# A convolution and two-layer feed-forward kernel on one core: w_in in three pieces, half 1's x by casting DMAs, the casts moved, seven blocks in halves

## The chip, the cores and the metric

One core of one Trainium2 chip. The metric is the device time of one execution, in microseconds (us). The kernel before: 693.57 us, median of three runs (692.63 to 694.27). PE is the matmul engine and PEld its weight load, DVE is VectorE, ACT ScalarE, POOL GpSimd, SP SyncE.

## The reference

```python
# x: (8, 4096, 192), weight: (8, 7), w_in: (192, 2048), w_out: (2048, 192)
w = softmax(weight, axis=-1)                      # 8 heads, 7 taps
x_pad = concat([zeros(8, 6, 192), x], axis=1)     # causal, padded in front
conv[b, s, h, :] = sum_k w[h, k] * x_pad[b, s + k, h, :]       # 24 channels a head
h = conv.reshape(32768, 192) @ w_in
out = maximum(0.01 * h, h) @ w_out                # (32768, 192), float32
```

## The kernel before

The 32768 rows are 32 blocks; a block is 512 positions of two batches (e = 0 and 1, one on each half of the partitions). For a block, VectorE convolves (three channel chunks c, seven taps each), PE multiplies by w_in (`mm1`, into the PSUM tile ph), ScalarE applies the leaky ReLU (into g), and PE multiplies g by w_out (`mm2`, into po), one group of blocks later. The first `NHALF` blocks go as two half groups of 256 positions each, so that the first matmuls can start early. A unit is the `mm1` work that fills one ph tile (in a half group, two of the 16 column groups of w_in, so that units 0 to 3 use its first half and units 4 to 7 its last); a step is two units and a share of `mm2`, four steps to a half group and eight to a full block.

In the head, before any of that runs, the softmax weights are made and block 0 is brought in by halves (q = 0 to 3 are the four halves of blocks 0 and 1). Two of half 0's three chunks are convolved on PE, with diagonal "tap matrices" (`diag`), and only the third on VectorE.

```python
    NHALF = 5                                  # blocks that go in halves
    groups = [(b, h * HT, HT) for b in range(NHALF) for h in range(2)]
    groups += [(b, 0, ST) for b in range(NHALF, NBLK)]
# [cut]
    def load_first(q):                         # [cut to its branches]
        # q 0, 1: float32 into x_nat on SyncE's queue (1 with rows interleaved), cast later on ACT or DVE
        # q 2:    casting DMA on GpSimd's queue into x_rows;   q 3: casting DMAs in chunks into x_half
# [cut]
    load_first(0)
    load_first(1)
# [cut: sel, built on GpSimd]
    w_in = [const_pool.tile([128, NCH, F // 2], BF16, name=f"w_in{h}") for h in range(2)]
    load_w_in(0, 0)                            # casting DMAs on GpSimd's queue, 64 partitions each
    ident = const_pool.tile([128, 128], BF16)
    make_identity(nc, ident)
    load_w_in(0, 1)
    for e in range(2):
        load_w_in(1, e)
    load_first(2)
    # then w_out, load_first(3), load_x(2), on the same queue
# [cut]
    select(wps_hm, slice(0, 2))                # tap weights: high and middle parts
    warm(3)                                    # matmuls on zeros
    select(wps_l, 2)                           # low part, another bank of the same tile
    warm(7)
    warm(1, 128)
    nc.vector.tensor_copy(out=whm, in_=wps_hm)
    diag_wide(0, 0, K)                         # tap matrices on VectorE
    cast_first(0, 0, nc.vector.tensor_copy)
    diag_low(0, range(2))                      # tap matrices on ScalarE
    cast_first(0, 1, nc.scalar.copy)
    transpose_first(0)
    warm(3)
# [cut: scalars, evacuation of half 0, the other tap matrices, the convolution of half 0]
        for u in range(2 * j, 2 * j + 2):
            mm1(grp, u)                        # unit u: two of the 16 column groups of w_in
            if i == 0 and u == 0:
                transpose_first(1)
                evac_first(1, nc.vector.tensor_copy, nc.vector.tensor_copy)
```

## Time and profile before

| | before |
|---|---|
| median time, span of the profiled run | 693.57 us, 692.1 us |
| PE busy | 684.0 us |
| first mm1 matmul that is not held up by w_in | 11.68 us |
| first mm2 matmul | 22.63 us |
| first full block starts, the next one | 116.18 us, 134.35 us |
| the last 160 mm2 matmuls start | 677.15 us |

A line of a timeline has the start in us, how long the group lasted from its first to its last instruction, the engine, the source line, what is written and read, the count, and in brackets the idle time just before it with what ended it. The timeline of GpSimd shows the queue of casting loads. A load is issued only after the load eight places before it has landed, so the waits tell landings:

```profile
1.86 0.76 POOL L253 DMA_DIRECT2D w_in<-in_moe_w_in_dram  x1
...
3.15 1.90 POOL L253 DMA_DIRECT2D w_in<-in_moe_w_in_dram  x3
...
9.63 0.72 POOL L134 DMA_DIRECT2D x_half<-in_x_dram  x1 [1.68 <-DMA w_in<-in_moe_w_in_dram]
11.92 0.72 POOL L134 DMA_DIRECT2D x_half<-in_x_dram  x1 [1.57 <-DMA w_in<-in_moe_w_in_dram]
13.81 0.72 POOL L134 DMA_DIRECT2D x_half<-in_x_dram  x1 [1.17 <-DMA w_in<-in_moe_w_in_dram]
15.67 1.43 POOL L134 DMA_DIRECT2D x_half<-in_x_dram  x2 [1.14 <-DMA w_in<-in_moe_w_in_dram]
```

The four loads of w_in landed a quarter microsecond before these lines: at about 9.4, 11.6, 13.5 and 15.4.

### The profile page before, as it was taken

The page shows a single profiled execution, that of the slowest core. Times are in us where ns is not written, and L with a number is a line of the kernel's source. Part 1 is how long each engine was busy: PE and PEld are TensorE (multiplying, and loading weights), DVE is VectorE, ACT ScalarE, POOL GpSimd, SP SyncE. Part 2 cuts the span into 40 slices and gives each one's busy share as a digit, 9 for nine tenths or more (in the row PEclk, how much of TensorE's full clock was granted, in tenths as well). Part 3 has the DMA queues.
Part 4 walks back from the last instruction along what each step waited for, and adds up shares of the span by engine and source line. Part 5 has one row for each costly group of instructions (what it writes and reads, how often), then busy time and mean ns, then how long its engine had stood idle before and what let it go on. Part 6 is the DMA issues. An engine that isn't in the chain of part 4 may idle for free.

```text
span 692.1 us, 26111 instructions
## 1 busy us (share of the span) xinstructions
PE 684.0 (99%) x11798; PEld 584.3 (84%) x11798; DVE 543.6 (79%) x1001; ACT 516.6 (75%) x575; POOL 144.6 (21%) x202
## 2 busy tenths in 40 slices
PE   8999999999999999999999999999999999999998
PEld 6999998788888888888888888888888888888887
DVE  6999999877878787878787878877878878787812
ACT  6888888977777777777777777777777777777771
POOL 6722220502222202222102222102222012000000
PEclk9999999999999999999999999999999999999999
DMA  9966644935565355566445565455665355222112
GB/s 181 107 84 94 83 70 71 93 71 75 66 93 81 69 81 72 71 90 85 68 76 76 75 82 85 73 76 70 83 81 79 74 74 67 70 60 59 48 42 65
DMA packets 183456, 54.00 MB, mean 78 GB/s; under 512 B 148528, under 2 KB 182576, under 8 KB 183344
## 3 DMA queue, kind: packets, MB, share of 16 engines
q0 software_dynamic: 98576, 14.56, 29.7%
q1 hardware_dynamic: 84768, 37.77, 23.0%
q8 instruction: 92, 1.51, 0.9%
q14 instruction: 20, 0.16, 0.1%
HBM read 29.88 MB, written 25.17 MB: 80 GB/s over the span
## 4 chain that ended last, share of the span: by engine, by line
PE 82%; DVE 14%; DMA 1%; ACT 1%; issue 1%; POOL 0%; POOLq 0%
PE po L432 42%; PE ph L403 40%; DVE yt L201 13%; DMA w_in<-in_moe_w_in_dram 1%; DVE yt L195 1%; ACT g L413 1%; DVE xt L176 0%; POOL w_in L253 0%; POOL sel L242 0%; DVE o_sb L479 0%; POOL sel L240 0%; PE ptr L156 0%; POOL ident masks.py:199 0%; POOL ident masks.py:197 0%; POOLq masks.py:199 0%
## 5 line engine op out<-in xcount | busy, mean ns | idle before, releaser
L413 ACT ACTIVATE g<-ph 128x1024 bf16<-128x1024 f32 x512 | 496.4, 1021 | 154.8 <-PE ph L403 154.3
L201 DVE SCALAR_TENSOR_TENSOR yt<-xt,wk,yt 128x512 bf16<-128x512 bf16 (+1 forms) x648 | 442.5, 683 | 17.7
L432 PEld LDWEIGHTS <-g 64*128 64x128 bf16 (+1 forms) x8064 | 361.0, 94 | 33.9 <-issue 0.2
L432 PE MATMUL po<-w_out,g 64*128 64x192 bf16 (+1 forms) x8064 | 387.5, 243 | 0.0
L403 PE MATMUL ph<-yt,w_in 64*128 64x512 bf16 (+1 forms) x3552 | 384.3, 347 | 3.1 <-DVE yt L201 1.3
L403 PEld LDWEIGHTS <-w_in 64*128 64x128 bf16 x3552 | 228.3, 111 | 65.7 <-issue 5.4
L79 POOL DMA_DIRECT2D x_bf<-in_x_dram x180 | 133.9, 770 | 427.1 <-DMA xt<-x_bf 318.1
L479 DVE COPY o_sb<-po 128x192 f32<-128x192 f32 x216 | 77.2, 358 | 122.6 <-PE po L432 115.6
L195 DVE TENSOR_SCALAR yt<-xt,wk 128x512 bf16<-128x512 bf16 (+1 forms) x108 | 38.4, 356 | 0.6 <-PE ph L403 0.5
L479 ACT COPY o_sb<-po 128x192 f32<-128x192 f32 x40 | 12.8, 320 | 2.1 <-PE po L432 0.2
L280 PE MATMUL warm<-zero 128*128 128x256 bf16 (+1 forms) x26 | 4.9, 340 | 1.1 <-DVE junk L237 1.1
L220 PE MATMUL acc<-xt,diag 64*64 64x256 bf16 x84 | 5.4, 271 | 0.4 <-ACT diag L342 0.4
L134 POOL DMA_DIRECT2D x_half<-in_x_dram x6 | 4.3, 714 | 5.6 <-DMA w_in<-in_moe_w_in_dram 5.6
L220 PEld LDWEIGHTS <-diag 64*64 64x64 bf16 x84 | 4.3, 106 | 1.3 <-DVE xt L176 0.6
L342 ACT ACTIVATE diag<-ident,whm 128x64 bf16<-128x64 bf16 x11 | 2.8, 339 | 2.1 <-DVE whm L328 2.1
L280 PEld LDWEIGHTS <-zero 128*128 128x128 bf16 x26 | 2.7, 118 | 2.1 <-DVE junk L237 1.1
L176 DVE COPY xt<-ptr 128x384 bf16<-128x384 bf16 x7 | 2.6, 416 | 1.4 <-PE ptr L156 1.4
L253 POOL DMA_DIRECT2D w_in<-in_moe_w_in_dram x4 | 2.7, 667 | 0.0
L368 ACT ACTIVATE yt<-acc,rsum 128x256 bf16<-128x256 f32 x3 | 1.4, 469 | 0.7 <-PE acc L220 0.7
L286 ACT ACT_TABLE_LOAD x1 | 1.3, 1283 | 0.8 <-PEq L572 0.8
L156 PE MATMUL ptr<-ident,x_half 64*128 64x64 bf16 x36 | 1.2, 190 | 0.6 <-DVE wraw L354 0.6
L140 ACT CAST x_half<-x_nat 128x384 bf16<-128x384 f32 x3 | 1.5, 503 | 0.3 <-DMA x_nat<-in_x_dram 0.3
(37 smaller groups left out, 13.0 us busy)
## 6 DMA issues: line engine op xcount, KB each, us to landing
out_dram<-o_sb SPq DMA_DIRECT2D x118, 192.0 KB, 2.1
x_bf<-in_x_dram POOLq DMA_DIRECT2D x180, 64.0 KB, 3.2
out_dram<-o_sb SPq DMA_DIRECT2D x20, 96.0 KB, 1.6
w_in<-in_moe_w_in_dram POOLq DMA_DIRECT2D x4, 384.0 KB, 9.1
xt<-x_bf SPq DMA_TRANSPOSE x90, 2.5
w_out<-in_moe_w_out_dram POOLq DMA_DIRECT2D x1, 768.0 KB, 13.7
x_nat<-in_x_dram SPq DMA_DIRECT2D x2, 192.0 KB, 2.5
x_nat<-in_x_dram SPq DMA_DIRECT2D x1, 384.0 KB, 7.5
```

The source lines that it names most:

```text
L79: nc.gpsimd.dma_start(out=t[:, c, :, e, :], in_=src[2 * rp + e, :, :, c * CH : (c + 1) * CH],)
L134: nc.gpsimd.dma_start(out=x_half[q][:, c, :, e, :], in_=rows[:, e, :, c * CH : (c + 1) * CH],)
L195: lambda s=src, d=dst, c=c: nc.vector.tensor_scalar_mul(d, s, wk[:, c, 0:1])
L201: lambda s=src, d=dst, c=c, k=k: nc.vector.scalar_tensor_tensor(out=d, in0=s, scalar=wk[:, c, k : k + 1], in1=d, op0=mybir.AluOpType.mult, ...
L220: lambda k=k, p=p, a=a, e=e, ps=ps: nc.tensor.matmul(out=acc[ps, :T], lhsT=diag[c][ps, p, k, :], rhs=xt[0][ps, c, a : a + T], start=(k == ...
L253: nc.gpsimd.dma_start(out=w_in[half][e * CH : (e + 1) * CH], in_=moe_w_in[:, fs].rearrange("(c p) f -> p c f", p=CH),)
L280: nc.tensor.matmul(out=wa[:, 0, 0:cols], lhsT=zero[:, 0:128], rhs=zero[:, 0:cols], start=True, stop=True,)
L342: nc.scalar.activation(out=diag[c][:, 1, k, :], in_=ident2, func=mybir.ActivationFunctionType.Copy, scale=whm[:, c, 1, k : k + 1],)
L403: nc.tensor.matmul(out=ph[:, e, i * T : (i + 1) * T], lhsT=w_in[f * 2 // NFC][ps, c, f // RUN % 2 * RUN * 128 + f % RUN : (f // RUN % 2 + ...
L413: act = nc.scalar.activation(out=g[blk][:, nf * u : nf * (u + 1), :, t0 : t0 + T], in_=ph.rearrange("p e (i t) -> p i e t", i=nf), func=my ...
L432: return nc.tensor.matmul(out=po[m], lhsT=g[b][ps, fc, e, s * 128 : (s + 1) * 128], rhs=w_out[ps, fc, :], start=start, stop=stop,)
L479: ins = copy(out=o_sb[:, n % 2, :], in_=po.pop(n))
```

## The change

The intent: get w_in's first columns sooner (a quarter instead of a half), take half 1's x and its casts away from ScalarE, do half 0's casts before anything that depends on the tap weights, and give VectorE four more half groups, in which it gains on PE, before the first full convolution.

```diff
-    NHALF = 5
+    NHALF = 7
 [cut: half 1 now takes half 2's path, a casting DMA into x_rows, then 24 transposes; its interleaved layout goes]
     load_first(0)
-    load_first(1)
 [cut]
-    w_in = [const_pool.tile([128, NCH, F // 2], BF16, name=f"w_in{h}") for h in range(2)]
+    pieces = (0, NFC // 4, NFC // 2, NFC)
+    w_in = [
+        const_pool.tile([128, NCH, (b - a) * 128], BF16, name=f"w_in{a}")
+        for a, b in zip(pieces[:-1], pieces[1:])
+    ]
 [cut: load_w_in and the slices of mm1 follow]
     load_w_in(0, 1)
-    for e in range(2):
-        load_w_in(1, e)
+    load_first(1)
+    for n in (1, 2):
+        for e in range(2):
+            load_w_in(n, e)
     load_first(2)
 [cut]
-    wps_l = wps[:, 1, 0 : NCH * (K + 1)].rearrange("p (c k) -> p c k", c=NCH)
+    wps_l = psum_o.tile([128, NCH, K + 1], FP32, name="wps_l", tag="po")
     select(wps_hm, slice(0, 2))
-    warm(3)
+    warm(1, 128)
     select(wps_l, 2)
-    warm(7)
-    warm(1, 128)
+    warm(6)
 [cut]
     diag_wide(0, 0, K)
-    cast_first(0, 0, nc.vector.tensor_copy)
+    for e in range(2):
+        cast_first(0, e, nc.scalar.copy)
     diag_low(0, range(2))
-    cast_first(0, 1, nc.scalar.copy)
     transpose_first(0)
 [cut: half 0 evacuated ahead of one small product; three tap matrices from VectorE to ScalarE;
       half 1's casts on ScalarE go; two more outputs are stored singly]
-                if i == 0 and u == 0:
+                if i == 0 and u == 1:
                     transpose_first(1)
```

More of the change, by code (lines that the diff above doesn't have):

```diff
@@ L43 @@
     NBLK = (B // 2) * NB
-    NHALF = 5
+    NHALF = 7
     RUN = 4
-    RUNS = 1
     NPEC = 2
@@ L109 @@
     x_half = {
-        q: const_pool.tile([128, NCH, HS, 2, CH], BF16, name=f"x_half{q}") for q in (0, 1, 3)
+        q: const_pool.tile([128, NCH, HS, 2, CH], BF16, name=f"x_half{q}") for q in (0, 3)
     }
-    x_rows = const_pool.tile([128, 2, HS, D], BF16, name="x_rows")
+    x_rows = {
+        q: const_pool.tile([128, 2, HS, D], BF16, name=f"x_rows{q}") for q in (1, 2)
+    }
     def load_first(q):
-        rows = x[0:2, q * HT : (q + 1) * HT, :].rearrange(
-            "e (p s) d -> p e s d" if q == RUNS else "e (s p) d -> p e s d", s=HS
-        )
-        if q < 2:
+        rows = x[0:2, q * HT : (q + 1) * HT, :].rearrange("e (s p) d -> p e s d", s=HS)
+        if q == 0:
             x_nat[q] = stage_pool.tile([128, 2, HS, D], FP32, name="x_nat")
-            if q == RUNS:
-                nc.sync.dma_start(
-                    out=x_nat[q].rearrange("p e s d -> p e (s d)"),
-                    in_=rows.rearrange("p e s d -> p e (s d)"),
-                )
-                return
             for e in range(2):
                 nc.sync.dma_start(out=x_nat[q][:, e], in_=rows[:, e])
-        elif q == 2:
+        elif q in x_rows:
             for e in range(2):
-                nc.gpsimd.dma_start(out=x_rows[:, e], in_=rows[:, e])
+                nc.gpsimd.dma_start(out=x_rows[q][:, e], in_=rows[:, e])
         else:
@@ L154, in transpose_first @@
                     ps = slice(i * CH, (i + 1) * CH)
-                    if q != 2:
+                    if q in x_half:
                         nc.tensor.transpose(
@@ L164, in transpose_first @@
                             out=ts[i][e * CH : (e + 1) * CH, s, c, :],
-                            in_=x_rows[ps, e, s, c * CH : (c + 1) * CH],
+                            in_=x_rows[q][ps, e, s, c * CH : (c + 1) * CH],
                             identity=ident[ps, ps],
@@ L171, in evac_first @@
         dst = xt[0][:, :, HALO + q * HT : HALO + (q + 1) * HT].rearrange(
-            "p c (i k s) -> p i s c k" if q == RUNS else "p c (s i k) -> p i s c k",
-            s=HS, i=2,
+            "p c (s i k) -> p i s c k", s=HS, i=2
         )
@@ L246, with load_w_in, w_in_of @@
         )
-    w_in = [const_pool.tile([128, NCH, F // 2], BF16, name=f"w_in{h}") for h in range(2)]
-    def load_w_in(half, e):
-        fs = slice(half * F // 2, (half + 1) * F // 2)
+    pieces = (0, NFC // 4, NFC // 2, NFC)
[3 more added lines that the diff above has]
+    ]
+    def load_w_in(n, e):
+        fs = slice(pieces[n] * 128, pieces[n + 1] * 128)
         nc.gpsimd.dma_start(
-            out=w_in[half][e * CH : (e + 1) * CH],
+            out=w_in[n][e * CH : (e + 1) * CH],
             in_=moe_w_in[:, fs].rearrange("(c p) f -> p c f", p=CH),
         )
+    def w_in_of(f, ps, c):
+        n = max(n for n in range(3) if pieces[n] <= f)
+        a = (f // RUN * RUN - pieces[n]) * 128 + f % RUN
+        return w_in[n][ps, c, a : a - f % RUN + RUN * 128 : RUN]
     load_w_in(0, 0)
@@ L358 @@
     nc.vector.reciprocal(rsum, rsum)
+    evac_first(0, nc.vector.tensor_copy, nc.scalar.copy)
     wk = const_pool.tile([128, NCH, K], FP32, name="wk")
     nc.vector.tensor_mul(wk, wraw[:, :, 0:K], rsum.to_broadcast([128, NCH, K]))
-    evac_first(0, nc.vector.tensor_copy, nc.scalar.copy)
     diag_low(0, range(2, K))
     diag_wide(1, 0, K)
-    diag_wide(1, 1, 3)
-    diag_low(1, range(3, K))
+    diag_low(1, range(K))
     def act_scale(out, in_, scale):
@@ L378 @@
         evac_y(act_scale)
-        cast_first(1, c, nc.scalar.copy)
         if c == 0:
@@ L390 @@
     LAST = NSUB - 2 * SUB
-    SINGLE = LAST - 12
+    SINGLE = LAST - 14
     def mm1(grp, u):
@@ L404, in mm1 @@
                         out=ph[:, e, i * T : (i + 1) * T],
-                        lhsT=w_in[f * 2 // NFC][
-                            ps, c, f // RUN % 2 * RUN * 128 + f % RUN
-                            : (f // RUN % 2 + 1) * RUN * 128 : RUN
-                        ],
+                        lhsT=w_in_of(f, ps, c),
                         rhs=y[ps, c, t0 : t0 + T],
```

## The prediction

> **What bounds the kernel now.** I read the page's busy shares and chain first, then the chain in order of time, then the timelines of the first 16 us and of the stretch around 116 us.
>
> ```profile
> PE 684.0 (99%) x11798; PEld 584.3 (84%) x11798; DVE 543.6 (79%) x1001; ACT 516.6 (75%) x575; POOL 144.6 (21%) x202
> ...
> PE 82%; DVE 14%; DMA 1%; ACT 1%; issue 1%; POOL 0%; POOLq 0%
> ```
>
> The kernel is a stream of matmuls. Work that the change doesn't touch sets most of the time: a full block needs 8 steps of 2.615 us (134.35 to 155.27 us in the timeline holds 8 steps: 20.92 us), and 32 such blocks are 669 us. The other 24 us of the 693.57 are the head before the first block, places where PE waits, and a tail. Only these can be won. The 14% of VectorE in the chain lie all before 118.5 us: up to there the convolution on VectorE runs without a pause, and PE keeps barely behind it.
>
> The chain in order of time, at the head:
>
> ```profile
> 3.15 8.48 DMA w_in<-in_moe_w_in_dram
> 11.63 0.05 issue
> 11.68 0.76 PE ph L403 x11
> 12.44 0.17 PE ptr L156 x8
> ...
> 12.72 1.06 DVE xt L176 x2
> 13.79 0.02 issue
> 13.81 0.30 DVE yt L195
> ```
>
> First matmuls of block 0 wait for the first half of w_in until 11.63; the transposes of half 1 stand behind them, and VectorE, done with half 0 at 11.3, sits until 12.71 for those transposes. But the load hides other work that ends just as late (timeline of the head):
>
> ```profile
> 4.64 0.21 DVE L328 COPY whm<-wps 128x48 f32<-128x48 f32 x1 [1.03 <-PE wps L316]
> 4.88 0.62 DVE L334 TENSOR_TENSOR diag<-ident,whm 128x448 bf16<-128x448 bf16 x1
> ...
> 5.37 0.49 ACT L140 CAST x_half<-x_nat 128x384 bf16<-128x384 f32 x1
> 5.42 0.54 DVE L140 CAST x_half<-x_nat 128x384 bf16<-128x384 f32 x1
> ...
> 8.23 3.09 DVE L201 SCALAR_TENSOR_TENSOR yt<-xt,wk,yt 128x256 bf16<-128x256 bf16 x6
> ...
> 10.99 0.47 ACT L368 ACTIVATE yt<-acc,rsum 128x256 bf16<-128x256 f32 x1 [0.71 <-PE acc L220]
> ```
>
> Even with w_in there at once, the second tap sum leaves ACT at 11.46 and VectorE's third of half 0 at 11.3: an earlier w_in **alone** is worth 0.2 us. The rest must come from the casts and tap matrices.
>
> The second place is the passage from half blocks to full ones (timeline of PE):
>
> ```profile
> 113.55 1.51 PE L403 MATMUL ph<-yt,w_in 64*128 64x256 bf16 x24
> 114.86 1.52 PE L432 MATMUL po<-w_out,g 64*128 64x192 bf16 x32
> 116.18 0.63 PE L403 MATMUL ph<-yt,w_in 64*128 64x512 bf16 x4
> 118.08 1.06 PE L403 MATMUL ph<-yt,w_in 64*128 64x512 bf16 x8 [1.27 <-DVE yt L201]
> ```
>
> PE stands 1.27 us for the first full convolution. The VectorE timeline has it starting at 102.81, its thirds at 107.97 and 112.95, and the end at 118.0: 15.2 us for a full one, while the last half group before it gives PE only four steps of 2.63 us, 10.52. VectorE had a lead of 105.66-102.81 = 2.85 us and needed 1.27 more.
>
> **What the Trainium skill says.** "TensorE: Matmul & The Clock Gate", Back-to-back issue gap: an isolated gap of N/2.4+2.5 ns when warm: 109 ns for 256 columns, 216 for 512. Here two row tiles run as a pair; 24 half matmuls take 1.31 us (113.55 to 114.86), 109 ns a pair, and 12 full ones 1.30 us (134.35 to 135.65), 216 a pair. The trace agrees, and going in halves costs PE only the 2.5 ns twice. "VectorE: DVE Perf Modes", The TRN2 errata: ops from SBUF pay a fixed extra latency per instruction. Here six 256-wide taps last 3.09 us (0.52 each), six 512-wide 4.69 us (0.78); the fixed part is 2x0.52-0.78 = 0.26 us, so halves burden VectorE. "DMA: Bandwidth & Descriptors", SWDGE vs HWDGE vs iDMA: a cast during a DMA goes only by GpSimd's path. So half 1's x now queues among w_in's pieces. Same page, Specifications: below 512 B a transfer loses line rate. The x rows land as 384 B, yet the trace shows little of it: last w_in piece at 4.41+11.0 = 15.4, both x_rows by 5.77+10.7 = 16.5, so 192 KB in about 1.1 us, against about 2.0 us for 384 KB of w_in (landings at 9.4, 11.6, 13.5, 15.4).
>
> **The change part by part.**
> 1. *Tap weights.* wps_l gets a tile of its own. Now the copy of whm waits 1.03 us for both selections, which share one tile; the first ended at 3.6 (3.26+0.33). The copy can go at 3.65, 1.0 us earlier; tap matrix 3.9 to 4.5, then four small ops (0.83 us together, from 5.89 to 6.72 now) until 5.4.
> 2. *Casts first.* Both go to ACT ahead of the tap matrices. x lands at about 3.8 and 4.3 (issues at 1.27 and 1.7 plus the 2.5 us in the DMA issues), so casts at 3.8 to 4.3 and 4.3 to 4.8 (0.50 each), the transposes at 4.9 to 5.3 (now 6.08 to 6.46), evacuated by 5.95 on ACT. PE's tap sums then start at 5.95 instead of 7.25 and last 3.7 us: 9.7 to 9.9. VectorE does its scalars, one tap matrix (0.62) and starts its third at 6.6 instead of 7.91: done at 10.0.
> 3. *ACT's load.* Three more tap matrices than now (14 against 11, 0.25 us each in a row), but half 1's two casts go (0.5 each), of which one stood between the two scalings. ACT: 12 tap matrices from 5.95 to 8.95, first scaling 9.4, second 9.9 to 10.4. So matmuls run freely from 10.45 instead of 11.68: **1.2 us earlier**.
> 4. *w_in in pieces.* Until 9.7 the queues now move 768 KB of x and 384 of w_in, some 0.18 MB/us from 3.0 on. With half as much of each, quarter 0 lands at about 7.3 (an estimate), half 1's x at 8.4, quarter 1 at 10.4, the last half at 14.4, half 2's x at 15.5, w_out at 19.2 (now 20.2). Needed at 10.5, 11.8, 12.3, 14.5, 18 and 21: in time, only the last half of w_in is tight.
> 5. *Half 1's transposes after two units.* Units of 0.66 us: 10.45 to 11.75, transposes (24, 0.38 us as half 2's now) to 12.1, copies 0.61 (half 2's now) instead of 1.06, whose target was interleaved. VectorE restarts convolving at 12.75 instead of 13.81: **1.05 us earlier**, and the first group that it bounds starts at 19.5 instead of 20.5. ACT's eight activations (0.98 each) have the same lead. From here PE and VectorE both run about **1.1 us** ahead of before.
> 6. *Seven blocks in halves.* Four more half groups. A convolution of a half takes 10.22, 10.22, 9.96, 9.97, 10.12 and 9.97 us in groups 4 to 9 (mean 10.08), PE 10.52: 0.44 us of lead each, 1.76 in all. Shortfall 1.27, so the wait at the passage goes, with 0.5 to spare. ACT's gap there falls from 1.75 us to its usual 0.33: **1.4 us** won. The passage itself (ACT bound for one block) stays. Cost: 16 steps of 2.630 instead of 2.615: 0.24 us.
> 7. *SINGLE.* One more pair of outputs goes out singly; SyncE isn't on the path: 0.
>
> Sum: 693.57 - 1.1 - 1.4 + 0.24 = **691.3 us**.
>
> **The rivals.**
> (a) *w_in's last half comes late.* Quarters mean 2 KB reads and 1 KB writes, and half 1's x is ahead of them; if it lands at 15.5, unit 4 waits 1 us and ACT idles. But VectorE's end at 19.5 hides about 0.5 of it. Head gain 0.5: 691.9.
> (b) *ACT's chain doesn't move.* If x lands late or its 14 tap matrices outlast the plan, units start at 11.0 or later and, as two stand ahead of the transposes instead of one, VectorE restarts hardly earlier: head gain 0.3: 692.1. For it: ACT is named in the waits of the head; against: it has gaps of 0.7 us at 10.3 and 0.65 at 5.9 now.
> (c) *The wait at the passage stays,* as VectorE gains less per half than I count (GpSimd's issues stretch its first op from 0.28 to 0.53). At 0.25 us a group the wait shrinks to 0.3: 691.6.
> (d) *More:* the lead at the head also removes the idle bits that PE has up to 22 us; perhaps 0.7 us: 690.6.
>
> **Range and chances.** Best case of all parts gives about 690, only the passage or only the head about 692.4; the runs of before spread by 1.6 us. So 690.1 to 692.7. No path moves 2% (14 us).
>
> **What would show it.** Right: matmuls with w_in starting at 10.2 to 10.8 and no wait on w_in after; VectorE's first op of half 1 near 12.8; no wait of PE on VectorE at the first full block (near 157 us); half steps of 2.63 us. Wrong: a wait on w_in at unit 2 or 4, VectorE idle over 1.5 us around 11, a wait of PE over 0.5 us at the passage, or a new idle stretch at w_out's first use near 21 us.

## The result

The changed kernel took 693.19 us (median of four runs, 692.58 to 694.74), the kernel before 693.83 us beside it; ratio 0.9997, 95% interval 0.9975 to 1.0018. In a later job with five more rounds it was 693.04 against 694.15, ratio 0.9988 (0.997 to 1.0005). A ratio is the mean time of one kernel's fast runs over that of the other's of the same rounds, so not quite the ratio of the medians. The profiled run has a span of 691.1 us, 1.0 less than before.

| | before | after | difference |
|---|---|---|---|
| first mm1 matmul that waits for nothing of half 0 | 11.68 | 11.18 | -0.50 |
| VectorE starts convolving half 1 | 13.81 | 13.59 | -0.22 |
| first mm2 matmul | 22.63 | 22.85 | +0.22 |
| first full block: from its start to the next one's | 18.17 | 16.71 | -1.46 |
| the last 160 mm2 matmuls start | 677.15 | 676.13 | -1.02 |

The sum closes: +0.22 in the head, -1.46 in the first full block, +0.24 for two blocks in halves (four half groups of 10.52 us for two full blocks of 20.92) make -1.00, against the -1.02 of the last line. The passage gave what was forecast. The head, forecast at -1.1, gave nothing.

The page of the changed kernel, its busy shares and its chain, by engine and by line:

```profile
PE 684.8 (99%) x11998; PEld 596.9 (86%) x11998; DVE 546.4 (79%) x1025; ACT 521.9 (76%) x593; POOL 147.2 (21%) x206
...
PE 96%; DMA 1%; ACT 1%; POOL 1%; issue 0%; DVE 0%; POOLq 0%
```

VectorE's 14% of the chain have gone to PE: VectorE is no longer behind anything. But the span moved by 0.15%. A chain's shares tell what was waited for last, not how long the waiting was: VectorE had been only just behind.

The chain in order of time, at the head:

```profile
7.09 9.69 DMA w_in<-in_moe_w_in_dram
16.78 0.05 issue
16.83 1.50 PE ph L402 x23
18.33 0.88 PE acc L212 x14
...
21.12 1.03 ACT g L409
22.15 0.04 issue
22.20 0.85 PE ph L402 x12
23.04 1.32 PE po L428 x32
```

Before, a load of w_in ended at 11.63 and VectorE set the pace from there. Now the chain waits for the *last* piece of w_in until 16.78, and 6.0 us after that the first mm2 matmul runs (22.85). The timeline of PE says the same, and shows a second loss ahead of it:

```profile
3.99 1.46 PE L282 MATMUL warm<-zero 128*128 128x256 bf16 x6
5.38 0.50 PE L149 MATMUL ptr<-ident,x_half 64*128 64x64 bf16 x12
5.81 0.82 PE L282 MATMUL warm<-zero 128*128 128x256 bf16 x3
6.56 2.07 PE L212 MATMUL acc<-xt,diag 64*64 64x256 bf16 x28
8.56 0.39 PE L282 MATMUL warm<-zero 128*128 128x256 bf16 x2
8.89 1.72 PE L212 MATMUL acc<-xt,diag 64*64 64x256 bf16 x28
...
16.83 1.50 PE L402 MATMUL ph<-yt,w_in 64*128 64x256 bf16 x23 [1.18 <-DMA w_in<-in_moe_w_in_dram]
```

The same three warm-up matmuls last 0.50 us in the kernel before (at 6.40) and 0.82 us here, the same 12 transposes 0.35 and 0.50, the same 28 tap sums 1.72 (at 7.25) and 2.07; the next 28 last 1.72 again. So PE was at a slow clock until about 7 us here and had left it by 4.5 to 5 before. The Trainium skill, "TensorE: Matmul & The Clock Gate", What's actually happening, says that PE starts at half its clock and is released after a busy window of some 3.4 us whose phase is not tied to the kernel. The durations fit such a halving. The cores view, a mean of 1.000 in both, does not show it, but the clock records kept with the traces do (not a view; in times from the span's start): the full clock was granted from 4.60 us in the kernel before, while the first trace of the changed kernel has no record. The window shows too: between two changes the clock stayed full for a whole number of 3.413 us (4 and 197 in casts_late below, 200 to 202 in the others).

The passage, timeline of PE; there is no wait where 1.27 us stood:

```profile
155.84 1.50 PE L402 MATMUL ph<-yt,w_in 64*128 64x256 bf16 x24
158.47 1.49 PE L402 MATMUL ph<-yt,w_in 64*128 64x512 bf16 x12
160.43 1.76 PE L402 MATMUL ph<-yt,w_in 64*128 64x512 bf16 x12
```

### The profile page after: what moved, and what is told of

The parts are those of the page before. It is cut to its first block, busy times and chain, and to the rows that moved or that the text cites. A ratio compares the mean times of both kernels' runs of the same rounds, so it can differ in the third digit from the quotient of the medians.

```text
span 691.1 us, 26558 instructions
## 1 busy us (share of the span) xinstructions
PE 684.8 (99%) x11998; PEld 596.9 (86%) x11998; DVE 546.4 (79%) x1025; ACT 521.9 (76%) x593; POOL 147.2 (21%) x206
## 3 DMA queue, kind: packets, MB, share of 16 engines
q1 hardware_dynamic: 84512, 37.38, 22.3%
## 4 chain that ended last, share of the span: by engine, by line
PE 96%; DMA 1%; ACT 1%; POOL 1%; issue 0%; DVE 0%; POOLq 0%
PE po L428 49%; PE ph L402 47%; DMA w_in<-in_moe_w_in_dram 1%; ACT g L409 1%; POOL w_in L248 0%; POOL x_rows L123 0%; PE acc L212 0%; POOL sel L233 0%; DVE o_sb L475 0%; PE ptr L156 0%; POOL ident masks.py:199 0%; POOL sel L231 0%; POOL ident masks.py:197 0%; PE ptr L149 0%; POOLq masks.py:199 0%
## 5 line engine op out<-in xcount | busy, mean ns | idle before, releaser
L193 DVE SCALAR_TENSOR_TENSOR yt<-xt,wk,yt 128x512 bf16<-128x512 bf16 (+1 forms) x684 | 450.5, 659 | 19.4
L402 PEld LDWEIGHTS <-w_in 64*128 64x128 bf16 x3744 | 240.6, 111 | 56.8 <-issue 3.2
L475 DVE COPY o_sb<-po 128x192 f32<-128x192 f32 x200 | 71.5, 358 | 113.7 <-PE po L428 108.0
L475 ACT COPY o_sb<-po 128x192 f32<-128x192 f32 x56 | 17.9, 319 | 3.1 <-PE po L428 0.2
L123 POOL DMA_DIRECT2D x_rows<-in_x_dram x4 | 2.9, 734 | 0.4 <-DMA w_in<-in_moe_w_in_dram 0.4
```

Source lines behind the costliest of these rows:

```text
L193: lambda s=src, d=dst, c=c, k=k: nc.vector.scalar_tensor_tensor(out=d, in0=s, scalar=wk[:, c, k : k + 1], in1=d, op0=mybir.AluOpType.mult, ...
L402: nc.tensor.matmul(out=ph[:, e, i * T : (i + 1) * T], lhsT=w_in_of(f, ps, c), rhs=y[ps, c, t0 : t0 + T], start=(c == 0), stop=(c == NCH - 1),)
L475: ins = copy(out=o_sb[:, n % 2, :], in_=po.pop(n))
```

## The experiments

Twelve runs were made, of ten new kernels (the changed kernel and halves came twice), in three jobs on three chips, each with the kernel before in its rounds. All were correct. The theories after the result: **load** (w_in's last half comes late, by smaller rows or by what is queued ahead of it), **clock** (PE is at its slow clock for longer), **passage** (seven blocks in halves win 1.2 us, whatever the head does). "Tap sums" is how long the first 28 took, 1.72 at full clock. "Last w_in" is the last load's issue plus its time to landing. "Wait" is PE's in all for w_in. "Full clock" is when the trace's clock records first have it (- where a trace has no record).

| run | median us | ratio to before | tap sums | last w_in | wait | first mm2 | full clock |
|---|---|---|---|---|---|---|---|
| before | 693.57 | | 1.72 | 15.4 | 0.5 | 22.63 | 4.60 |
| before7 | 693.58 | 0.9995 (0.9982 to 1.0007) | 1.72 | 16.6 | 1.5 | 23.67 | 6.33 |
| after | 693.19 | 0.9997 (0.9975 to 1.0018) | 2.07 | 16.8 | 1.2 | 22.85 | - |
| after_again | 693.04 | 0.9988 (0.997 to 1.0005) | 3.19 | 16.7 | 0 | 24.73 | 12.32 |
| nhalf5 | 693.41 | 0.9989 (0.9977 to 1.0002) | 3.06 | 16.7 | 0.2 | 23.01 | 9.36 |
| x1_sync | 693.1 | 0.9988 (0.9976 to 1.0001) | 2.14 | 15.8 | 0 | 22.16 | 7.46 |
| both | 693.95 | 1.0 (0.9983 to 1.0018) | 2.99 | 16.4 | 0 | 23.02 | 9.22 |
| warm | 693.22 | 0.9986 (0.9969 to 1.0003) | 1.72 | 17.4 | 1.8 | 23.49 | 5.18 |
| halves | 692.24 | 0.9977 (0.9963 to 0.9991) | 2.62 | 15.8 | 0 | 23.38 | 9.26 |
| halves_again | 692.92 | 0.9986 (0.9971 to 1.0001) | 3.19 | 16.2 | 0 | 23.40 | 10.02 |
| halves_warm | 692.2 | 0.9977 (0.9966 to 0.9989) | 1.72 | 16.0 | 0 | 22.45 | - |
| hwarm_u0 | 692.39 | 0.9977 (0.9966 to 0.9989) | 1.72 | 15.7 | 0 | 22.12 | 5.80 |
| casts_late | 692.67 | 0.9996 (0.9978 to 1.0015) | 1.72 | 17.7 | 2.5 | 25.42 | 4.48 |
| halves_early | 696.2 | 1.0026 (1.0011 to 1.0042) | 3.19 | 14.3 | 0 | 26.07 | 13.46 |

A profile is of one run; the spans of one kernel in one job differ by up to 3.9 us (the kernel before in after_again's job: 691.0 to 694.9), so one row's head is not a median's.

### The passage: nhalf5 and before7

```diff
 nhalf5, on the changed kernel          before7, on the kernel before
-    NHALF = 7                          -    NHALF = 5
+    NHALF = 5                          +    NHALF = 7
```

> The changed kernel with five blocks in halves instead of seven. If the passage is what seven blocks win: PE waits about 0.9 to 1.3 us for VectorE at the first full block near 116 us again, and the span is 0.7 to 1.2 us longer than the changed kernel's, about 692. Rival (the wait would have gone through the head's change alone): no wait there, span about 690.9.

> The kernel before with seven blocks in halves, nothing else. If the passage alone carries the gain: no wait of PE at the first full block near 158 us, the passage block 16.7 us instead of 18.2, 0.24 us paid for the longer steps, span about 690.9, or 1.2 us less than the kernel before's, as good as the whole change or 0.2 better. Rival (halves gain nothing without the new head): a wait over 0.5 us stays.

Timeline of PE in nhalf5: the wait is back.

```profile
116.56 0.63 PE L402 MATMUL ph<-yt,w_in 64*128 64x512 bf16 x4
118.21 1.06 PE L402 MATMUL ph<-yt,w_in 64*128 64x512 bf16 x8 [1.02 <-DVE yt L193]
```

In before7 it is gone: the first full block starts at 159.30 with no idle time ahead of its matmuls. Its start is 135.63 us after the first mm2 matmul, and 135.62 in the changed kernel, so the stretch from there is the same with either head. Its span is only 0.2 us shorter than that of the kernel before, as in this run the first half of w_in came 1.0 us later (PE waits 1.54 us for it, until 12.72) and took back what the passage gave. So the passage theory holds in the traces, and in all of them: from the first mm2 matmul to the last 160 it is 653.3 to 653.9 us in the twelve profiles with seven blocks in halves, 654.3 and 654.5 in the two with five. The times don't show it: before7's spans average 691.9 against 692.3 for the kernel before in the same rounds, not 1.2 less, and nhalf5's average 691.5, the changed kernel's ten 691.6. Why the unprofiled runs show so little of it is open.

### The load: halves, halves_again, x1_sync, both

```diff
 halves, halves_again
-    pieces = (0, NFC // 4, NFC // 2, NFC)
+    pieces = (0, NFC // 2, NFC)
-    for n in (1, 2):
+    for n in (1,):
 x1_sync: half 1's x as before (SyncE's queue, float32, ScalarE casts), w_in in quarters and a half
     load_first(0)
+    load_first(1)
 both: halves and x1_sync together
```

> The changed kernel with w_in in two halves again, all else kept. Small-rows theory (a quarter writes 1 KB rows and moves at some 110 to 130 KB/us, a half writes 2 KB rows at some 190): the first half lands at about 8.5 us, half 1's x at 9.6, the last half at about 14 instead of 16.8, so the matmuls with w_in have no wait of 1.2 us on it; the first mm2 matmul comes at about 21.8 instead of 22.85 and the span falls by about 1 us to about 690. Queue-order theory (half 1's x ahead of the rest of w_in makes it late): the last half still lands at 16 or later and the wait stays.

> The changed kernel with w_in in two halves, once more, for comparison in the same rounds. If packets of 2 KB for 1 KB are what w_in gains: last half by 15.9 again, no wait of PE on w_in; ratio to the kernel before 0.997 to 0.9985 and a span of 690.3 to 691.9, the longer ones where x comes late or the clock is slow. If the first time was luck: ratio 0.999 or more.

> The changed kernel with half 1's x as fp32 through SyncE's queue and cast on ACT as in the kernel before, w_in still in quarters and a half. Queue-order theory: without the 192 KB of x ahead of it w_in's last half lands 1.1 to 1.6 us sooner, 15.2 to 15.7, and the wait of 1.2 us at unit 4 shrinks to 0.3 or less. Small-rows theory: the quarters stay slow and twice the bytes of x share the engines, so the last half lands at 16.5 to 18 and the wait stays at 1 us or more; the span is the changed kernel's or up to 1 us more.

> The changed kernel with all of its loads undone: w_in in two halves and half 1's x through SyncE and cast on ACT; the casts ahead of the tap matrices, the two units ahead of the transposes and seven blocks in halves stay. If the loads set the head: the first half of w_in lands at 11.3 to 12.7 as in the kernel before, the matmuls with w_in wait for it, no wait on the last half, and the first mm2 matmul comes at 22.3 to 23.7, no sooner than before; span 690.8 to 692. If the reordered compute gains by itself: first mm2 matmul at 21.8 or sooner, span about 690.3.

With w_in in two halves the last half landed at 15.8, 16.2, 16.0 and 15.7 in four profiles, with quarters at 16.8, 16.7, 16.7, 17.4 and 17.7 in five: means of 15.9 and 17.1. PE waits for w_in in four of the five and in none of the four; the late clock hides a wait in both runs of halves, but hwarm_u0, whose free matmuls start at 11.27 as against the changed kernel's 11.18, has none either. The forecasts of 8.5 and 14 were too early even so (the first half landed at 10.3), and the first mm2 matmul, forecast at 21.8, came at 23.38. halves_again's ratio, 0.9986, lies between the two bands that were forecast.

The 1.2 us are lost ahead of the last half: the first half and half 1's x had landed by 11.6 to 12.4, the two quarters and x by 12.4 to 13.7. Why quarters are slower is shown only in part. In the trace's DMA packets (not a view, but counted from its records) the two quarters are 768 packets of 1 KB, of 114 to 125 ns each on average. The first half, in the same place of the queue, is 384 packets of 2 KB, of 208 to 237 ns. (In the last half, later, 2 KB take only 174 to 178.) Over 16 DMA engines that is about 5.7 us (768 x 119 / 16) against 5.3 (384 x 222 / 16), 0.4 of the 1.2, and a rough estimate, as the busy share of an engine goes up to 1.4 there, so that packets overlap. That quarters are also six loads instead of four was not tested apart.

x1_sync goes against the small-rows theory as it stood: with the quarters kept, and only half 1's x out of GpSimd's queue, the last half landed at 15.8 and PE's wait was gone, nearly what the queue-order theory said. Timeline of PE, where the wait of 1.18 us stood:

```profile
14.83 2.81 PE L413 MATMUL ph<-yt,w_in 64*128 64x256 bf16 x36
```

In the changed kernel half 1's x landed 1.0 us after the first quarter (9.6 after 8.6), and 1.0 us is what its going gave. So **either** undoing removed the wait (x1_sync in its one profile); together, in both, the loads landed no sooner (16.4, and 15.4 and 16.6 in the two kernels with the old loads). Why they don't add is open; the old loads alone scatter by 1.2 us. There is also a limit that I had not counted: GpSimd's queue is slow at first. In two profiles of the changed kernel it moves 75 to 190 KB/us from 4 to 9 us, with SyncE's queue empty, and about 200 only from 12 us on; in the kernel before it moves 84 to 137 from 4 to 8 us with SyncE's moving 49 to 123 beside it, and about 200 from 10 on. The engines were not left idle by the x taken off SyncE's queue: from 4 to 9 us their busy share was 0.86 to 1.38 in the changed kernel's first trace and 0.95 to 1.11 in the kernel before. They moved fewer bytes in that time.

both gained nothing (ratio 1.0), with the new order of compute and with seven blocks in halves. That fits the theory that the loads set the head only in part: the wait for the first half, forecast with it, did not come, as that half landed at 11.2 and the late clock (tap sums of 2.99 us) let the free matmuls start at 12.10 only.

### The clock: after_again, warm, halves_warm

```diff
 warm, on the changed kernel; halves_warm, on halves
     select(wps_hm, slice(0, 2))
-    warm(1, 128)
+    warm(3)
     select(wps_l, 2)
-    warm(6)
+    warm(7)
+    warm(1, 128)
```

> The changed kernel once more, for a ratio over five rounds and a second look at its head. If the first result was typical: ratio to the kernel before 0.998 to 1.000, span 690.5 to 692.5, the last half of w_in lands at 16.2 to 17.2 and PE waits for it at unit 4 unless its first unit is late, and PE's tap sums still start at the slow clock (28 of them in 2.0 us or more against 1.72). If that was bad luck: tap sums in 1.75 us or less, w_in's last half before 15.8, span under 690.5.

> The changed kernel with the warm-up matmuls between and after the two selections put back as in the kernel before (3 and 8 instead of 1 and 6). Warm-up theory (fewer and shorter warm-ups put off the full clock from 4.4 to 6.1 us to 7 to 9.5): full clock before 6.5, first 28 tap sums in 1.72 to 1.75 us, matmuls with w_in from 10.2 to 10.9; yet the last half of w_in still lands at 16 to 17 and PE waits 1.2 to 2 us for it, so the span stays at 690.5 to 691.5. Rival (only the phase of the clock's window against the start differs from run to run): the full clock comes at 7 to 9.5 as in the four runs with the new head.

> w_in in two halves and the warm-up matmuls between and after the selections put back. If load and clock together took the head's gain: full clock before 6.5, matmuls with w_in from 10.2 to 11.0, no wait on w_in over 0.5 us, first mm2 matmul at 21.5 to 22.3, spans of 689.8 to 690.6 with little scatter, ratio 0.996 to 0.997. Rival (something else holds the head): first mm2 matmul at 22.8 or later.

after_again was worse luck than the first look: the timeline of ScalarE shows the second half of half 0's x landing at 5.5 us instead of 4.4, the tap sums ran at the slow clock to beyond 10 us, and the first mm2 matmul came 1.9 us later than in the first profile.

```profile
5.51 0.51 ACT L133 CAST x_half<-x_nat 128x384 bf16<-128x384 f32 x1 [1.21 <-DMA x_nat<-in_x_dram]
```

No wait for w_in is left in that run, as everything else was later still. So two profiles of the changed kernel show two different heads. Its spans scatter accordingly (691.1, 690.6, 691.5, 693.0 and 693.2, 692.6, 690.5, 690.7, 691.1, 691.6), but so do those of the kernel before (691.0 to 694.9), and what the unprofiled ones owe to the head is not known.

With the warm-ups put back the first tap sums took 1.72 us in three of three kernels (as in both kernels with the old head). With the shorter ones they took 2.07 to 3.19 us in eight of nine profiles, and 1.72 in one (casts_late). The theory holds as a tendency: fewer warm-ups make a late clock likelier; they don't decide it. The clock records tell what else does. The changes fall on borders 3.41 us apart (the window above), which lie differently in each run. In hwarm_u0 the full clock came at the border at 5.80. With the shorter warm-ups, in both, halves and nhalf5, it did not come at the borders at 5.81, 5.85 and 5.95 (one window before the change on record) but at the next, 9.22, 9.26 and 9.36; in casts_late it came at 4.48. So neither the warm-ups nor where the borders lie settles the clock alone.

In warm the clock was right, the matmuls ran from 10.96, and PE then waited 0.7 us for the second quarter and 1.06 for the last half: the first mm2 matmul came at 23.49, 6.0 us after w_in's landing, as in the first profile. Halves alone had the load right, the clock wrong: 23.38 and 23.40. halves and halves_warm separate the clock cleanly: their tap sums start at 7.37 and 7.33 and last 2.62 and 1.72 us, 0.90 of the 0.93 us between their first mm2 matmuls. Both put right:

```profile
7.33 1.72 PE L212 MATMUL acc<-xt,diag 64*64 64x256 bf16 x28
...
11.60 1.39 PE L403 MATMUL ph<-yt,w_in 64*128 64x256 bf16 x22 [0.34 <-ACT yt L369]
...
22.45 1.52 PE L429 MATMUL po<-w_out,g 64*128 64x192 bf16 x32
```

This is halves_warm's timeline of PE: no wait for w_in, the first mm2 matmul at 22.45, and five spans from 690.2 to 690.9 (halves_again, in the same rounds: 689.9 to 692.8). The expected 21.5 to 22.3 was not quite met, nor the ratio of 0.996 to 0.997: the warm-ups themselves, at the slow clock until 6.2, held the transposes back to 6.23. So even with load and clock put right the head is only 0.2 us ahead of the kernel before's profile (22.63), not 1.1.

### Sooner, and in another order: halves_early, hwarm_u0, casts_late

```diff
 halves_early, on halves: GpSimd's first load of w_in ahead of the three instructions that make sel
 hwarm_u0, on halves_warm
-                if i == 0 and u == 1:
+                if i == 0 and u == 0:
 casts_late, on the changed kernel
-    for e in range(2):
-        cast_first(0, e, nc.scalar.copy)
+    cast_first(0, 0, nc.vector.tensor_copy)
     diag_low(0, range(2))
+    cast_first(0, 1, nc.scalar.copy)
```

> The changed kernel with w_in in two halves and its first load issued ahead of GpSimd's three instructions that build sel, at 0.8 us instead of 1.85. If the queue of casting loads sets the head: its data start 1 us sooner, the first half of w_in lands at about 9.3, the last at about 14.8 instead of 15.75, no wait on either; the first mm2 matmul at 21.5 to 22.3 with the matmuls with w_in from 10.6 to 11.4; span 689.8 to 690.6, ratio to the kernel before about 0.996. If compute and the clock set it: the landing moves but the first mm2 matmul stays at 22.8 or later.

> As halves_warm, with half 1's transposes after the first unit again instead of after two. If VectorE's restart bounds the first groups: it restarts 0.6 us sooner and the first mm2 matmul comes 0.2 to 0.5 us sooner than in halves_warm. If ScalarE's eight activations bound them: an idle bit of ScalarE after the first activation and the first mm2 matmul the same or up to 0.3 us later.

> The changed kernel with half 0's casts back in their old places, the first on VectorE behind the wide tap matrix and the second on ScalarE behind two low ones. If w_in's last half bounds the head: the transposes come 0.5 us later, the matmuls with w_in up to 0.5 us later, but the first mm2 matmul stays at 22.5 to 23.0 as the wait for w_in absorbs it; span 690.8 to 691.5. If the casts' place counts: first mm2 matmul at 23.2 or later.

halves_early is the only kernel slower than the one before beyond doubt. Its last half of w_in landed at 14.3, the soonest of all, and yet its median is 2.05 us above that of the kernel before in the same rounds (694.15), where halves was 1.69 below its own (693.93). The timeline of ScalarE tells why:

```profile
3.93 0.51 ACT L133 CAST x_half<-x_nat 128x384 bf16<-128x384 f32 x1 [1.17 <-DMA x_nat<-in_x_dram]
...
7.04 0.51 ACT L133 CAST x_half<-x_nat 128x384 bf16<-128x384 f32 x1 [2.60 <-DMA x_nat<-in_x_dram]
```

The first packets of w_in started at 2.93 us instead of about 3.6, beside those of half 0's x, and x's second half landed at 7.0 instead of 4.4. The Trainium skill, "DMA: Bandwidth & Descriptors", Queues, rings and completion order, has each DMA engine alternating between queues, packet by packet; the trace agrees in so far as the earlier stream delayed the later one. PE then idled for 2 us and ran slow: the tap sums took 3.19 us, the first mm2 matmul came at 26.07. The same race may lie behind the late x of halves and after_again, but that is not shown: w_in's first packets began at 3.49 and 3.52 us there and x's last packet at 5.24 and 4.97; where w_in began at 3.53 or later x's last packet came at 4.05 at most. A border of 0.01 us in profiles of different runs is no proof.

hwarm_u0: VectorE starts convolving half 1 sooner and the first mm2 matmul comes at 22.12, 0.33 before halves_warm's. As expected for VectorE's restart; but its first free mm1 matmul was also 0.33 sooner (11.27 for 11.60), so nothing is shown for the order itself. Its ratio is the same.

casts_late missed: the transposes came at 5.11, *earlier* than the 5.38 of the changed kernel. The place of the casts is not the reason: they were done at 4.96 on VectorE and 5.00 on ScalarE, and at 4.96 with both on ScalarE. So the new place gains nothing, and the 0.27 us are the clock's, full from 4.48 here: the six warm-ups ahead of the transposes lasted 1.05 us, 1.46 in the changed kernel. The matmuls ran from 10.3, the soonest of all, and waited for every piece of w_in after the first quarter. Timeline of PE:

```profile
16.17 0.30 PE L402 MATMUL ph<-yt,w_in 64*128 64x256 bf16 x1 [0.92 <-DMA w_in<-in_moe_w_in_dram]
17.78 2.48 PE L402 MATMUL ph<-yt,w_in 64*128 64x256 bf16 x23 [1.32 <-DMA w_in<-in_moe_w_in_dram]
20.20 1.59 PE L212 MATMUL acc<-xt,diag 64*64 64x256 bf16 x14
```

These 23 matmuls took 1.50 us in the changed kernel and the 14 tap sums 0.95. The windows view has the reason. In a line stand the stretch, the busy times of the engines, and last the granted clock, the busy share of the DMA engines and KB/us:

```profile
17.00:18.00 1.00, 0.22 (x4) 0.22 (x6) 0.93 (x3) 0.00 (x0) 0.13 (x1) 1.00 1.18 210
...
19.00:20.00 1.00, 1.00 (x11) 0.59 (x7) 0.46 (x1) 0.98 (x1) 1.00 (x2) 0.50 1.46 180
...
22.00:23.00 1.00, 1.00 (x40) 0.76 (x36) 0.08 (x1) 0.70 (x2) 0.29 (x1) 1.00 0.31 18
```

PE was back at half its clock, from 18.13 to 21.55 by the clock records, after 3.4 us in which two waits of 0.92 and 1.32 us had broken up its work. So the wait was paid twice, and the first mm2 matmul came at 25.42. Two of this kernel's six runs have a span of 693.7 and 694.0, with a mean granted clock of 0.998, the others 690.7 to 691.1, with 0.999 or more.

Best of the versions tried are halves_warm and hwarm_u0: 0.9977 of the kernel before, interval below 1, where the changed kernel's intervals hold 1. (halves had 0.9977 once and 0.9986 again; the times alone don't separate it from them.) They didn't run in the same rounds as the changed kernel, so their lead over it, about 1 us by spans, rests on the ratios and on the profile.

## Why the prediction was wrong

- **Step 1, tap weights: right.** The copy of whm came at 3.63 (forecast 3.65), the tap matrix at 3.88, the small operations ended at 5.47 (5.4).
- **Step 2, casts first: half right, and this step failed on the clock.** The casts ran from 3.85 to 4.96. But I took transposes and tap sums at the durations of the kernel before. The six warm-ups lasted 1.46 us and the transposes started at 5.38 instead of 4.9; the tap sums ran from 6.56 to 10.6 instead of 5.95 to 9.9. The free matmuls came at 11.18, not 10.45: 0.73 us lost. With the full clock from 4.48, in casts_late, they came at 10.32, with the casts in their old place. That fewer warm-ups could put off the full clock was in the diff, and no rival named it. Nor did I see that ScalarE with two casts is no faster than two engines with one each.
- **Step 3, ScalarE's load: right.** Twelve tap matrices from 6.32 to 9.29, 3.0 us as forecast; the second scaling then waited for PE (1.00 us), not the reverse.
- **Step 4, w_in in pieces: this step failed most, on the size of the quarters.** By landings the first quarter came at 8.6 (forecast 7.3), half 1's x at 9.6 (8.4), the second quarter at 12.9 (10.4) and the last half at 16.8 (14.4). So x took 1.0 us and the last half 3.9, as forecast (1.1 and 4.0); the quarters make up the 2.4 us, the first 1.3 late, the second 3.3 us instead of 2.0. I took 384 KB as 2.0 us in any row size, though the loads measured were in 2 KB rows, and I took it that SyncE's bytes, once gone, would be GpSimd's to use: 0.18 MB/us, where the queue moved 0.10 to 0.19 from 4 to 9 us. The step had every piece in time; PE waited 1.18 us. Rival (a) named this wait with a landing of 15.5; it was short by 1.3.
- **Step 5, transposes after two units: failed with its inputs.** VectorE restarted at 13.59, forecast 12.75. The copies took 0.62 us as forecast. From the free mm1 matmul to the first mm2 matmul it was 11.67 us, 11.08 by the forecast; 10.91 in x1_sync, where PE doesn't wait for w_in. The head missed its forecast by 1.32 us (+0.22 for -1.1): 0.73 of them lie before the free matmuls, with the late clock, and 0.59 after them, with the wait.
- **Step 6, seven blocks in halves: right to 0.1 us in the profiles.** -1.46 and +0.24.
- **Step 7: right.** The last 160 matmuls took 12.00 us in both.
- **The range** was set as if the two parts were independent of the run. Neither the scatter of x's and w_in's arrivals (15.4 and 16.6 for the same loads in before and before7) nor that of the clock was in it. The profile's span fell by 1.0 us, the median by 0.6.

What was shown: the late quarters and PE's wait (traces, and the absence of the wait with either load undone), the late clock and its cost (halves against halves_warm, and the clock records), and the passage (both ways, in the traces). That the head gains only when load and clock are both right is too strong: x1_sync, with the full clock from 7.46, had its first mm2 matmul at 22.16, as soon as hwarm_u0. What stays open: what makes the quarters slow besides their packets, why halves and x1_sync don't add, why GpSimd's queue is slow for its first 6 us, and why the times show so little of the passage.

## What to carry to other kernels

When a load is cut up so that its first part arrives sooner, compute when the **last** part arrives, at the packet size that the cut leaves and with everything that now shares its queue; here the first part landed 3.0 us sooner (8.6 for 11.6), of which the matmuls used 0.5, and the last 1.4 us later (16.8 for 15.4), for which PE waited 1.18. A head of some ten microseconds has its own clock and its own races: taking filler matmuls out, or starting a stream sooner, can slow what it was to speed up. When one engine is on the chain for 14% of the span, look for the one place where it is really waited for, as little more than that wait (1.27 us here; the passage became 1.46 shorter) can be won.

## What the Trainium skill lacked or had wrong

- "TensorE: Matmul & The Clock Gate", What you observe, puts the change to the full clock at around 4 us of sustained activity, give or take 0.5. In these heads, where PE issues matmuls from 1.12 us on with short pauses, it came between 4.48 and 13.46 us. And in casts_late the clock fell back to half for 3.413 us although no pause of PE in the 3.4 us before was longer than 1.32 us.
- "DMA: Bandwidth & Descriptors" has no rate for the first microseconds of casting loads on GpSimd's queue: 75 to 190 KB/us here from 4 to 9 us, about 200 from 12 on, and on average 114 to 125 ns for a packet of 1 KB, 174 to 237 for one of 2 KB.
- The same page, Issuing engines are not separate DMA queues, says that issuing from several engines only saves issue time. In the head, with both queues at work, more was moved per microsecond (208 to 249 KB/us at 5 to 8 us in the kernel before) than by GpSimd's queue alone (98 to 165 KB/us at 5 to 8 us in the changed kernel). The loads differ in kind, as SyncE's don't cast, so this is a hint and no test.
- No page warns that a casting stream started 0.7 us sooner can put off a load of another queue by 2.6 us (half 0's x, from 4.4 to 7.0).
